# Retention and a squared-ReLU FFN on one core: from a batch at a time to 36 units of 128 tokens with FFN groups of 512

## The chip, the core and the metric

The kernel runs on one core of a Trainium2 chip. The metric is device time in microseconds. Before the change it is 639.69 us, the median of 3 runs (639.65 to 640.98). Five engines work side by side, each on its own queue of instructions in program order: TensorE (PE, with its weight loads shown apart as PEld), VectorE (DVE), ScalarE (ACT), GpSimd (POOL) and SyncE (SP), which here only issues DMAs.

## The reference

Eight batches of eight heads, 576 tokens, head size 64. Retention has no softmax: scores are multiplied by a decay that falls with the distance of the tokens. An FFN with a squared ReLU follows on all 4608 tokens.

```python
gamma = 1.0 - 2.0 ** (-5.0 - np.arange(H))
Dmat = np.where(rel >= 0, gamma[:, None, None] ** rel, 0.0)   # rel = i - j
ret = (q @ k.T / sqrt(64) * Dmat) @ v                          # per batch and head
x = ret.transpose(0, 2, 1, 3).reshape(4608, 512)
h = x @ w_in                                                   # 512 -> 2048
out = (np.maximum(h, 0) ** 2) @ w_out                          # 2048 -> 512
```

## The kernel before

Everything is computed in fp16 with fp32 sums in PSUM. The retention is done in chunks of 128 tokens: inside a chunk by masked scores, across chunks by a 64x64 state per head.

The loop over the 8 batches (L100) has three stages.

1. **Retention** (L103 to L197), one head at a time. Six DMAs load q, k and v of the head with runs of 256 bytes (L110 to L122). ACT and DVE cast them and multiply q and k by their decays (L124 to L143). PE transposes q and k together, five matmuls (L150); ACT copies qT out (L153) and DVE kT (L154). Five score matmuls follow (L165), four state matmuls (L170), the mask on DVE (L174) with the running state (L179, L181), and per chunk an output matmul from the masked scores (L188) and one from the state (L192) with ACT's copy into xT (L195). A head has 64 rows, so most of these matmuls use half of PE's rows or half of its columns.
2. **FFN1** (L201 to L213): 16 blocks of 128 hidden columns times two halves of 288 tokens, four matmuls each (L205); ACT takes the ReLU (L210), POOL squares it (L212).
3. **FFN2** (L215 to L226): five token tiles, 16 matmuls of 512 columns each (L219), DVE's copy (L224), and a DMA of SP (L225).

A scheduler places the instructions; on PE the stages follow one another, save that the next head's transposes and the next stage's first matmuls begin a little early. The weights are loaded in fp32 through SP and cast by POOL (L90) and DVE (L97) at the start, beside the first heads.

Of the kernel before, what the change touches and what calls it, by code (L numbers as in the profile page):

```python
# [8 lines left out]
FP32 = mybir.dt.float32  # L9
FP16 = mybir.dt.float16  # L10


@with_exitstack
def kernel(
# [5 lines left out]
    moe_w_in: bass.AP,  # L20
    moe_w_out: bass.AP,
    out: bass.AP,
):
    nc = tc.nc
    B, H, S, D = q.shape
    DM, DFF = moe_w_in.shape
    assert (B, H, S, D) == (8, 8, 576, 64)
    scale = 1.0 / math.sqrt(D)

    NQ = 288  # L30
    n_kt = (S + 127) // 128
    n_ic = S // NQ
    n_f = DFF // 128
    n_dm = DM // 128
    n_tt = (S + 127) // 128
    C = 128

    const_pool = ctx.enter_context(tc.tile_pool(name="const", bufs=1))
    w_pool = ctx.enter_context(tc.tile_pool(name="w", bufs=1))
    stage_pool = ctx.enter_context(tc.tile_pool(name="stage", bufs=2))  # L40
    qk_pool = ctx.enter_context(tc.tile_pool(name="qk", bufs=3))
    work_pool = ctx.enter_context(tc.tile_pool(name="work", bufs=2))
    big_pool = ctx.enter_context(tc.tile_pool(name="big", bufs=1))
    psum_pool = ctx.enter_context(tc.tile_pool(name="psum", bufs=8, space=bass.MemoryType.PSUM))

    identity_h = const_pool.tile([128, 128], FP16, name="identity_h")
    make_identity(nc, identity_h)

    iota_p = const_pool.tile([128, 1], FP32, name="iota_p")
    nc.gpsimd.iota(iota_p, pattern=[[0, 1]], base=0, channel_multiplier=1,  # L50
                   allow_small_or_imprecise_dtypes=True)
    one_p = const_pool.tile([128, 1], FP32, name="one_p")
    nc.vector.memset(one_p, 1.0)

    qdecay = []
    kdecay = []
    dmask = []
    gummas = []
    for h in range(H):
        gamma = 1.0 - 2.0 ** (-5.0 - h)  # L60
        lng = math.log(gamma)
        gummas.append(gamma)
        qd = const_pool.tile([128, 1], FP32, name=f"qdecay{h}")
        kd = const_pool.tile([128, 1], FP32, name=f"kdecay{h}")
        mbias = stage_pool.tile([128, 1], FP32, name=f"mb{h}", tag="mb")
        nc.vector.memset(mbias, math.log(scale))
        nc.scalar.activation(out=qd, in_=iota_p,
                             func=mybir.ActivationFunctionType.Exp,
                             bias=mbias, scale=lng)
        mbias2 = stage_pool.tile([128, 1], FP32, name=f"mb2{h}", tag="mb")  # L70
        nc.vector.memset(mbias2, 128.0 * lng)
        nc.scalar.activation(out=kd, in_=iota_p,  # L72
                             func=mybir.ActivationFunctionType.Exp,
                             bias=mbias2, scale=-lng)
        dm_t = const_pool.tile([128, C], FP32, name=f"dmask{h}")
        nc.gpsimd.memset(dm_t, gamma ** -128)
        nc.gpsimd.affine_select(
            out=dm_t, in_=dm_t, compare_op=mybir.AluOpType.is_ge, fill=0.0,
            base=0, pattern=[[1, C]], channel_multiplier=-1,
        )  # L80
        qdecay.append(qd)
        kdecay.append(kd)
        dmask.append(dm_t)

    w_in_h = []
    for dm in range(n_dm):
        st = stage_pool.tile([128, DFF], FP32, name=f"w_in_st{dm}", tag="wst")
        nc.sync.dma_start(out=st, in_=moe_w_in[dm * 128:(dm + 1) * 128, :])
        t = w_pool.tile([128, DFF], FP16, name=f"w_in{dm}")
        nc.gpsimd.tensor_copy(out=t, in_=st)  # L90
        w_in_h.append(t)
    w_out_h = []
    for f in range(n_f):
        st = stage_pool.tile([128, DM], FP32, name=f"w_out_st{f}", tag="wst2")
        nc.sync.dma_start(out=st, in_=moe_w_out[f * 128:(f + 1) * 128, :])
        t = w_pool.tile([128, DM], FP16, name=f"w_out{f}")
        nc.vector.tensor_copy(out=t, in_=st)  # L97
        w_out_h.append(t)
# [158 lines left out]
```

## Time and profile before

The table is from one profiled execution, taken on the only core. Its span, from first to last instruction, is 638.2 us; an own end-to-end time of that execution is not listed. The median of the timed runs, 639.69 us, is 1.5 us above the span.

| | PE | PEld | DVE | ACT | POOL |
|---|---|---|---|---|---|
| busy us | 517.0 | 299.2 | 201.4 | 303.6 | 172.7 |
| share of the span | 81% | 47% | 32% | 48% | 27% |
| instructions | 3136 | 3136 | 841 | 913 | 283 |

The chain of work that ended last runs 58% through PE, 22% through POOL, 7% through ACT and 6% through DVE. DMA moved 46.76 MB, 73 GB/s over the span; 117696 of its 124913 packets are under 512 bytes.

PE's busy time counts each matmul from its start to its modelled end, so overlapping matmuls in a row are merged and a busy PE need not stream columns at its peak. Mean times of one matmul therefore hold a fixed tail; how fast a row of matmuls goes is read from a timeline row: its length less the mean of the last one, over the count less one.

### The profile page before, as it was taken

What the parts mean: (1) busy time and instruction counts of PE and PEld (TensorE: products, weight loads), DVE (VectorE), ACT (ScalarE), POOL (GpSimd) and SP (SyncE); (2) the same over time, 40 slices, a digit from 0 to 9 for tenths busy, and PEclk for the clock granted to TensorE, in tenths of its full rate; (3) what the DMA queues carried; (4) which work ended last, traced back from release to release, by engine and by line L of the source; (5) the groups of instructions that cost most, each with busy time, mean ns of one, the idle gap of its engine ahead of it and who ended that gap; (6) DMA issues with size and microseconds to landing.
All of it is one profiled execution on the core that took longest, in us unless ns stands there. A gap on an engine that the chain in (4) does not pass through costs nothing.

```text
span 638.2 us, 9634 instructions
## 1 busy us (share of the span) xinstructions
PE 517.0 (81%) x3136; PEld 299.2 (47%) x3136; DVE 201.4 (32%) x841; ACT 303.6 (48%) x913; POOL 172.7 (27%) x283
## 2 busy tenths in 40 slices
PE   0357998779977899779987799877997789977997
PEld 0234644447444564446544475444744446444563
DVE  2555114440154302551035501444015530254101
ACT  3255733566146660566425563366614566055450
POOL 4200750009200290005700075000930019000380
PEclk9999998559975599557995579755997559965699
DMA  7765502430133301432024310233113330120001
GB/s 286 230 162 125 115 35 69 91 86 20 50 81 84 85 1 66 91 86 57 17 67 94 90 32 34 69 85 90 24 49 76 90 84 1 66 66 0 1 13 62
DMA packets 124913, 46.76 MB, mean 73 GB/s; under 512 B 117696, under 2 KB 117696, under 8 KB 124352
## 3 DMA queue, kind: packets, MB, share of 16 engines
q1 hardware_dynamic: 124864, 46.17, 27.7%
q8 instruction: 24, 0.39, 0.3%
q14 instruction: 25, 0.20, 0.1%
HBM read 36.70 MB, written 9.44 MB: 72 GB/s over the span
## 4 chain that ended last, share of the span: by engine, by line
PE 58%; POOL 22%; ACT 7%; DVE 6%; DMA 4%; issue 2%; ACTq 0%; SPq 0%; DVEq 0%
POOL gT L212 22%; PE pout L219 18%; PE pout L188 9%; PE pout L192 8%; PE ps_sc L165 7%; PE ptr L150 7%; ACT qT L153 6%; PE ph L205 5%; DVE kT L154 5%; PE ps_st L170 3%; DMA w_out_st<-in_moe_w_out_dram 3%; DVE w_out L97 1%; ACT r L210 1%; DMA qk<-in_k_dram 1%; DVE retT L174 0%
## 5 line engine op out<-in xcount | busy, mean ns | idle before, releaser
L212 POOL TENSOR_TENSOR gT<-r 128x288 f16<-128x288 f16 x256 | 161.2, 670 | 438.9 <-ACT r L210 438.3
L219 PE MATMUL pout<-w_out,gT 128*128 128x512 f16 (+1 forms) x640 | 142.9, 380 | 7.5 <-POOL gT L212 6.9
L205 PE MATMUL ph<-xT,w_in 128*128 128x288 f16 x1024 | 143.2, 306 | 0.0
L210 ACT ACTIVATE r<-ph 128x288 f16<-128x288 f32 x256 | 105.3, 411 | 59.7 <-POOL gT L212 41.6
L205 PEld LDWEIGHTS <-w_in 128*128 128x128 f16 x1024 | 104.9, 104 | 33.0
L165 PE MATMUL ps_sc<-qT,kT 64*128 64x128 f16 (+1 forms) x320 | 48.9, 286 | 80.9 <-DVE kT L154 79.6
L224 DVE COPY o<-pout 128x512 f32<-128x512 f32 (+1 forms) x40 | 27.6, 690 | 270.5 <-PE pout L219 270.5
L219 PEld LDWEIGHTS <-gT 128*128 128x128 f16 (+1 forms) x640 | 62.8, 100 | 85.5 <-POOL gT L212 13.6
L153 ACT COPY qT<-ptr 64x576 f16<-64x576 f16 x64 | 40.5, 632 | 129.9 <-PE ptr L150 129.4
L188 PE MATMUL pout<-retT,vh 128*64 128x128 f16 (+1 forms) x320 | 90.1, 282 | 3.2 <-ACT xT L195 0.7
L195 ACT CAST xT<-pout 64x128 f16<-64x128 f32 (+1 forms) x320 | 75.0, 246 | 33.5 <-PE pout L188 19.1
L174 DVE TENSOR_TENSOR retT<-ps_sc,dmask 128x128 f16<-128x128 f32 (+1 forms) x320 | 79.8, 266 | 24.5 <-PE ps_sc L165 24.5
L150 PE MATMUL ptr<-identity_h,qkh 128*128 128x128 f16 (+1 forms) x320 | 55.5, 274 | 25.5 <-ACT kdecay L72 13.0
L165 PEld LDWEIGHTS <-kT 64*128 64x128 f16 (+1 forms) x320 | 28.7, 123 | 101.0 <-DVE kT L154 89.0
L192 PE MATMUL pout<-qT,state 64*64 64x128 f16 (+1 forms) x256 | 73.9, 292 | 0.0
L128 ACT ACTIVATE qkh<-qk,qdecay 128x256 f16<-128x256 f32 x64 | 32.4, 507 | 82.6 <-PE ps_st L170 82.5
L154 DVE COPY kT<-ptr 64x576 f16<-64x576 f16 x64 | 29.4, 459 | 106.2 <-ACT qT L153 106.2
L192 PEld LDWEIGHTS <-state 64*64 64x64 f16 x256 | 31.8, 124 | 50.3 <-issue 33.5
L150 PEld LDWEIGHTS <-qkh 128*128 128x128 f16 (+1 forms) x320 | 27.1, 113 | 45.2 <-issue 16.1
L188 PEld LDWEIGHTS <-vh 128*64 128x64 f16 (+1 forms) x320 | 39.0, 140 | 15.5 <-DVE retT L174 0.3
L181 DVE SCALAR_TENSOR_TENSOR state<-state,ps_st 64x64 f16<-64x64 f16 x192 | 39.6, 206 | 0.0
L170 PE MATMUL ps_st<-vh,qkh 128*64 128x64 f16 x256 | 26.3, 241 | 0.0
(24 smaller groups left out, 160.7 us busy)
## 6 DMA issues: line engine op xcount, KB each, us to landing
qk<-in_q_dram SPq DMA_DIRECT2D x64, 128.0 KB, 2.3
qk<-in_k_dram SPq DMA_DIRECT2D x64, 128.0 KB, 2.5
v<-in_v_dram SPq DMA_DIRECT2D x64, 128.0 KB, 2.4
out_dram<-o SPq DMA_DIRECT2D x32, 256.0 KB, 2.0
w_in_st<-in_moe_w_in_dram SPq DMA_DIRECT2D x4, 1024.0 KB, 5.9
w_out_st<-in_moe_w_out_dram SPq DMA_DIRECT2D x16, 256.0 KB, 2.9
qk<-in_q_dram SPq DMA_DIRECT2D x64, 16.0 KB, 2.2
qk<-in_k_dram SPq DMA_DIRECT2D x64, 16.0 KB, 2.2
```

The source lines that it names most:

```text
L150: nc.tensor.transpose(ptr[:, st * C:st * C + slen], qkh_sb[0:slen, st, :], identity_h[0:slen, 0:slen])
L153: nc.scalar.copy(out=qT_h, in_=ptr[0:64, :])
L154: nc.vector.tensor_copy(out=kT_h, in_=ptr[64:128, :])
L165: nc.tensor.matmul(ps_sc[i][0:L, 0:L], lhsT=kT_h[:, i * C:i * C + L], rhs=qT_h[:, i * C:i * C + L], start=True, stop=True)
L174: nc.vector.tensor_tensor(out=retT[0:L, i * C:i * C + L], in0=ps_sc[i][0:L, 0:L], in1=dmask[h][0:L, 0:L], op=mybir.AluOpType.mult)
L188: nc.tensor.matmul(pout[:, 0:L], lhsT=vh_sb[0:L, i, :], rhs=retT[0:L, i * C:i * C + L], start=True, stop=(i == 0))
L192: nc.tensor.matmul(pout[:, 0:L], lhsT=states[i - 1], rhs=qT_h[:, i * C:i * C + L], start=False, stop=True)
L195: nc.scalar.copy(out=xT_h[dm][hodd * 64:hodd * 64 + 64, i * C:i * C + L], in_=pout[:, 0:L])
L205: nc.tensor.matmul(ph, lhsT=w_in_h[dm][:, f * 128:(f + 1) * 128], rhs=xT_h[dm][:, ic * NQ:ic * NQ + NQ], start=(dm == 0), stop=(dm == n_dm ...
L210: nc.scalar.activation(out=r_sb, in_=ph, func=mybir.ActivationFunctionType.Relu)
L212: nc.gpsimd.tensor_tensor(out=gT_sb[f][:, ic * NQ:ic * NQ + NQ], in0=r_sb, in1=r_sb, op=mybir.AluOpType.mult)
L219: nc.tensor.matmul(pout[0:tlen, :], lhsT=gT_sb[f][:, t * 128:t * 128 + tlen], rhs=w_out_h[f], start=(f == 0), stop=(f == n_f - 1))
```

## The change

The kernel is rewritten. The work is cut into 36 units of 128 tokens of all 8 heads: four full chunks per batch, and one tail unit for two batches, which holds the last 64 tokens of each. Four units make a group of 512 tokens, and there are 9 groups.

A unit's retention works on pairs of heads, so that stationary operands are 128x128. kT is kept twice with the other head's rows zeroed (`kTs`), v is padded with zero columns (`vps`), and the state of a pair is a 128x128 matrix whose off-diagonal blocks the constant `bdec` zeroes. The decay moves: v is multiplied on POOL, the mask is 0 or 1, and the query side's decay is multiplied in when the output leaves PSUM (`gam`). Each unit has 8 transposes, 8 scores, 4 state matmuls (none in a tail) and, per pair, 2 output matmuls and 1 from the state (none in a batch's first chunk, 2 of 64 columns in a tail).

POOL casts k and q; ACT copies kT out of PSUM in two halves; DVE copies qT, masks four score blocks at a time, carries the state and squares the ReLU. The FFN output is copied by ACT and sent by ACT's DMA queue. The weights come by eight DMAs of POOL's queue that cast to fp16 on the way.

The order is written out by hand (`manual_schedule`): the four units of group 0 first, one after the other; then, for each group, its 64 FFN1 and 64 FFN2 matmuls, and between them the retention of the next group's units, each unit within 32 FFN matmuls: one transpose, score or state matmul after an FFN matmul, three output matmuls after each from the 27th on. Removed lines are those printed above; the core of the new ones:

```diff
+    units = []
+    for bp in range(B // 2):
+        for b in (2 * bp, 2 * bp + 1):
+            units += [("full", b, c) for c in range(4)]
+        units.append(("tail", 2 * bp, 4))
+    NU = len(units)
+    UPG = 4
+    NG = NU // UPG
...
+    ld = ctx.enter_context(tc.tile_pool(name="ld", bufs=5))
+    cast = ctx.enter_context(tc.tile_pool(name="cast", bufs=3))
+    work = ctx.enter_context(tc.tile_pool(name="work", bufs=2))
+    st_pool = ctx.enter_context(tc.tile_pool(name="st", bufs=4))
...
+    ps_ff = ctx.enter_context(tc.tile_pool(name="ps_ff", bufs=3, space=bass.MemoryType.PSUM))
+    ps_sc = ctx.enter_context(tc.tile_pool(name="ps_sc", bufs=2, space=bass.MemoryType.PSUM))
+    ps_one = ctx.enter_context(tc.tile_pool(name="ps_one", bufs=1, space=bass.MemoryType.PSUM))
+    ctx.enter_context(tc.manual_schedule())
...
+    def load(u):
+        kind, b, c = units[u]
+        t = {}
+        for name, src in (("q", q), ("k", k), ("v", v)):
+            x = ld.tile([P, H, D], FP32, name=f"{name}32", tag=f"{name}32")
+            if kind == "full":
+                nc.sync.dma_start(out=x, in_=src[b, :, c * P:(c + 1) * P, :].rearrange("h p d -> p h d"))
+            else:
+                for i in range(2):
+                    nc.sync.dma_start(out=x[i * 64:(i + 1) * 64],
+                                      in_=src[b + i, :, 512:576, :].rearrange("h p d -> p h d"))
+            t[name] = x
+        loaded[u] = t
...
+    for u in range(4):
+        load(u)
+    for fb in range(4):
+        nc.gpsimd.dma_start(out=w_in16[:, :, fb * 512:(fb + 1) * 512],
+                            in_=w_in[:, fb * 512:(fb + 1) * 512].rearrange("(m p) f -> p m f", p=P))
+    for fb in range(4):
+        nc.gpsimd.dma_start(out=w_out16[:, fb * 4:(fb + 1) * 4, :],
+                            in_=w_out[fb * 512:(fb + 1) * 512, :].rearrange("(n p) m -> p n m", p=P))
...
+    ident = const.tile([P, P], FP16, name="ident")
+    make_identity(nc, ident)
...
+        m = const.tile([P, P], FP32, name=f"mask_{kind}")
+        nc.gpsimd.memset(m, 1.0)
+        nc.gpsimd.affine_select(out=m, in_=m, compare_op=ALU.is_ge, fill=0.0,
+                                base=0, pattern=[[1, P]], channel_multiplier=-1)
...
+        t = const.tile([P, NP, 192], FP16, name=f"vp{i}")
+        nc.vector.memset(t[:, :, 64:128], 0.0)
+        vps.append(t)
+        t = const.tile([P, NP, 2, P], FP16, name=f"kTb{i}")
+        nc.vector.memset(t[64:128, :, 0, :], 0.0)
+        nc.vector.memset(t[0:64, :, 1, :], 0.0)
...
+        nc.gpsimd.tensor_copy(out=k16, in_=t["k"].rearrange("p h d -> p (h d)"))
+        nc.gpsimd.tensor_copy(out=q16, in_=t["q"].rearrange("p h d -> p (h d)"))
+        vp = vps[u % NB]
+        vo = vp.rearrange("p n (a d) -> p n a d", d=64)[:, :, 0:3:2, :]
+        nc.gpsimd.tensor_tensor(
+            out=vo,
+            in0=t["v"].rearrange("p (n a) d -> p n a d", a=2),
+            in1=vdec[kind].rearrange("p (n a o) -> p n a o", a=2, o=1).to_broadcast([P, NP, 2, D]),
+            op=ALU.mult)
...
+                    nc.tensor.transpose(ps[:, i, hp, :], r[src][:, hp * P:(hp + 1) * P], ident)
+                    if hp == NP - 1:
+                        if i == 1:
+                            kT = kTs[u % NB]
+                            qT = work.tile([P, NP, P], FP16, name="qT", tag="qT")
+                            nc.scalar.copy(out=kT[0:64, :, 0, :], in_=ps[0:64, 0])
+                            nc.scalar.copy(out=kT[64:128, :, 1, :], in_=ps[64:128, 0])
+                            nc.vector.tensor_copy(out=qT, in_=ps[:, 1])
...
+                    if hp % 2 == 0 and a == 0:
+                        r["psc"] = ps_sc.tile([P, 2, 2, P], FP32, name="psc", tag="psc")
+                    nc.tensor.matmul(r["psc"][:, hp % 2, a, :], lhsT=r["kT"][:, hp, a, :],
+                                     rhs=r["qT"][:, hp, :], start=True, stop=True)
+                    if hp % 2 == 1 and a == 1:
+                        nc.vector.tensor_tensor(
+                            out=rT[:, hp - 1:hp + 1].rearrange("p n a i -> p (n a) i"),
+                            in0=r["psc"].rearrange("p n a i -> p (n a) i"),
+                            in1=mask[kind].rearrange("p (o i) -> p o i", o=1).to_broadcast([P, 4, P]),
+                            op=ALU.mult)
...
+                    if c == 0:
+                        nc.vector.tensor_tensor(out=Rn, in0=psf, in1=bdec, op=ALU.mult)
+                    else:
+                        tmp = work.tile([P, NP, P], FP32, name="stmp", tag="stmp")
+                        nc.vector.tensor_tensor(out=tmp, in0=psf, in1=R[b], op=ALU.add)
+                        nc.vector.tensor_tensor(out=Rn, in0=tmp, in1=bdec, op=ALU.mult)
...
+        inter = [] if c == 0 else ([(0, P, R[b])] if kind == "full" else [(0, 64, R[b]), (64, P, R[b + 1])])
...
+                    nc.tensor.matmul(r["psO"][:, hp, :], lhsT=r["vp"][:, hp, a * 64:a * 64 + P],
+                                     rhs=r["rT"][:, hp, a, :], start=(a == 0),
+                                     stop=(a == 1 and not inter))
...
+                    nc.tensor.matmul(r["psO"][:, hp, lo:hi], lhsT=Rb[:, hp, :], rhs=r["qT"][:, hp, lo:hi],
+                                     start=False, stop=last)
...
+            nc.vector.tensor_tensor(out=xTs[g][:, :, s * P:(s + 1) * P], in0=r["psO"], in1=gam[kind], op=ALU.mult)
...
+                    nc.tensor.matmul(cur["ph"], lhsT=w_in16[:, m, f * P:(f + 1) * P], rhs=xTs[g][:, m, :],
+                                     start=(m == 0), stop=(m == NP - 1))
+                    if m == NP - 1:
+                        gT.append(g_pool.tile([P, UPG * P], FP16, name=f"gT{f}", tag=f"gT{f}"))
+                        rl = r_pool.tile([P, UPG * P], FP16, name="rl", tag="rl")
+                        nc.scalar.activation(out=rl, in_=cur["ph"], func=ACTF.Relu)
+                        nc.vector.tensor_tensor(out=gT[f], in0=rl, in1=rl, op=ALU.mult)
...
+                    nc.tensor.matmul(cur["po"], lhsT=gT[f][:, t * P:(t + 1) * P], rhs=w_out16[:, f, :],
+                                     start=(f == 0), stop=(f == NF - 1))
+                    if f == NF - 1:
+                        o = work.tile([P, DM], FP32, name="o", tag="o")
+                        nc.scalar.copy(out=o, in_=cur["po"])
+                        if kind == "full":
+                            r0 = b * S + c * P
+                            nc.scalar.dma_start(out=out[r0:r0 + P, :], in_=o)
...
+    for u in range(UPG):
+        cast_unit(u)
+        run(steps_T(u))
+        run(steps_score(u))
+        run(steps_state(u))
+        run(steps_out(u))
+    for g in range(NG):
+        nxt = [u for u in range((g + 1) * UPG, (g + 2) * UPG) if u < NU]
+        wide = 2 * NF * UPG
+        per = wide // UPG
+        w_steps = steps_ff1(g)
+        w2 = None
+        queue = []
+        for i in range(wide):
+            if i == NF * NP:
+                w_steps += steps_ff2(g)
+            slot, ph = divmod(i, per)
+            if nxt:
+                if ph == 0:
+                    u = nxt[slot]
+                    load(u)
+                    cast_unit(u)
+                if ph == 2:
+                    queue += steps_T(nxt[slot])
+                if ph == 14:
+                    queue += steps_score(nxt[slot])
+                    queue += steps_state(nxt[slot])
+                if ph == 27:
+                    queue += steps_out(nxt[slot])
+            w_steps[i]()
+            if queue:
+                queue.pop(0)()
+            if ph >= 27 and queue:
+                queue.pop(0)()
+                if queue:
+                    queue.pop(0)()
+        run(queue)
```

On PE, before, the end of a head: the last output matmuls of a head from the masked scores (vh) and from the state, and behind them the next head's first transpose.

```order
L188 LDWEIGHTS vh
L188 MATMUL pout<-retT,vh 64x64
L192 LDWEIGHTS state_517
L192 MATMUL pout<-qT,state_517 64x64
L150 LDWEIGHTS qkh
L150 MATMUL ptr<-identity_h,qkh 128x128
```

On PE now, in the first group's FFN2 (po, from gT and w_out): a state matmul (psS) of the next group's unit stands between two FFN matmuls.

```order
L310 LDWEIGHTS gT_515
L310 MATMUL po<-w_out_88,gT_515 128x512
L229 LDWEIGHTS k_777
L229 MATMUL psS<-vp_191,k_777 128x128
L310 LDWEIGHTS gT_535
L310 MATMUL po<-w_out_88,gT_535 128x512
```

Retention matmuls stood in chains of their own; now FFN matmuls of 512 columns lie between them, of the group before.

On PE now, at the end of that group: the last unit's last output matmuls (psO), the group's last FFN2 matmul (po), and the next group's first FFN1 matmul, which waits for DVE's xT.

```order
L257 LDWEIGHTS vp_191
L257 MATMUL psO<-rT,vp_191 128x128
L263 LDWEIGHTS R
L263 MATMUL psO<-qT,R 128x128
L310 LDWEIGHTS gT_667
L310 MATMUL po<-w_out_88,gT_667 128x512
L290 LDWEIGHTS w_in_87
L290 MATMUL ph<-xT,w_in_87 128x512 [waits DVE_49]
```

Between the output that DVE must turn into xT and the matmul that reads it stands one FFN2 matmul.

On POOL, before, the constants come first and the casts of the weights wait for SP's DMAs; the end of the constants:

```order
L77 AFFINE_SELECT dmask_159<-dmask_159 128x128 [waits Pool_49]
L77 AFFINE_SELECT dmask_170<-dmask_170 128x128 [waits Pool_49]
L90 CAST w_in_175<-w_in_st_173 128x2048 [waits DMAHW0_49]
L90 CAST w_in_179<-w_in_st_177 128x2048 [waits DMAHW1_49]
L90 CAST w_in_183<-w_in_st_181 128x2048 [waits DMAHW0_49]
```

On POOL now, the start: the eight weight DMAs, then the constants (ident is what the transposes need), then the first unit's casts.

```order
L82 DMA w_in_87<-in_moe_w_in_dram 128x4x512 x4
L85 DMA w_out_88<-in_moe_w_out_dram 128x4x512 x4
masks.py:197 MEMSET ident 128x128
masks.py:199 ISA
masks.py:199 AFFINE_SELECT ident<-ident 128x128 [waits Pool_49]
L92 IOTA iota_p 128x1
L95 IOTA iota_f 128x128
```

The identity, and with it the first transpose, has moved behind eight DMA issues on the same queue.

## Rows read from the trace of the kernel before

**Rows 1.** Page, part 2: TensorE's granted clock in tenths, 40 slices

```profile
PEclk9999998559975599557995579755997559965699
```

**Rows 2.** Stages of a batch: window, length, busy per engine, clock, DMA, GB/s

```profile
253.52:292.71 39.19, 28.83 (x184) 16.22 (x184) 21.21 (x97) 23.21 (x76) 0.00 (x0) 0.56 0.37 83
292.71:310.05 17.34, 17.34 (x131) 13.02 (x130) 0.00 (x0) 11.42 (x30) 14.98 (x24) 0.92 0.12 26
310.05:328.86 18.81, 17.83 (x82) 7.77 (x80) 2.77 (x4) 2.88 (x7) 5.12 (x9) 1.00 0.15 57
```

**Rows 3.** Waits: who <- for whom: us in total, times, longest

```profile
ACT r L210 <- POOL gT L212: 41.6, 193, 0.3
PE ps_sc L165 <- DVE kT L154: 79.6, 63, 1.6
```

**Rows 4.** Groups by shape: busy us, mean ns of one | idle before, releasers

```profile
L212 POOL TENSOR_TENSOR gT<-r 128x288 f16<-128x288 f16 x256 | 161.2, 670 | 438.9 <-ACT r L210 438.3
L219 PE MATMUL pout<-w_out,gT 128*128 128x512 f16 x512 | 114.4, 379 | 7.5 <-POOL gT L212 6.9
L210 ACT ACTIVATE r<-ph 128x288 f16<-128x288 f32 x256 | 105.3, 411 | 59.7 <-POOL gT L212 41.6 <-PE ph L205 17.2
L195 ACT CAST xT<-pout 64x128 f16<-64x128 f32 x256 | 62.6, 256 | 28.2 <-PE pout L188 19.1 <-PE pout L192 6.8
L153 ACT COPY qT<-ptr 64x576 f16<-64x576 f16 x64 | 40.5, 632 | 129.9 <-PE ptr L150 129.4
L154 DVE COPY kT<-ptr 64x576 f16<-64x576 f16 x64 | 29.4, 459 | 106.2 <-ACT qT L153 106.2
L224 DVE COPY o<-pout 128x512 f32<-128x512 f32 x32 | 22.1, 692 | 247.5 <-PE pout L219 247.5
L90 POOL CAST w_in<-w_in_st 128x2048 f16<-128x2048 f32 x4 | 7.6, 1894 | 8.1 <-DMA w_in_st<-in_moe_w_in_dram 8.1
```

**Rows 5.** Timeline, PE in both FFN stages: start, us, engine, line, count

```profile
299.82 3.35 PE L205 MATMUL ph<-xT,w_in 128*128 128x288 f16 x26
...
325.74 3.18 PE L219 MATMUL pout<-w_out,gT 128*64 128x512 f16 x14
```

**Rows 6.** Timeline, a batch's first two heads, clock 1.00, then 0.50

```profile
328.86 0.53 PE L150 MATMUL ptr<-identity_h,qkh 128*128 128x128 f16 x5
...
329.42 0.63 ACT L153 COPY qT<-ptr 64x576 f16<-64x576 f16 x1 [15.05 <-PE ptr L150]
330.09 0.46 DVE L154 COPY kT<-ptr 64x576 f16<-64x576 f16 x1 [0.44 <-ACT qT L153]
...
330.60 0.54 PE L165 MATMUL ps_sc<-qT,kT 64*128 64x128 f16 x5 [1.22 <-DVE kT L154]
...
334.73 0.79 PE L165 MATMUL ps_sc<-qT,kT 64*128 64x128 f16 x5 [1.22 <-DVE kT L154]
```

**Rows 7.** Groups by shape, 328.5 to 329.5 us: last of five transposes

```profile
L150 PE MATMUL ptr<-identity_h,qkh 64*128 64x64 f16 x1 | 0.2, 200 | 0.0
```

**Rows 8.** Timeline of the first 23 us

```profile
0.80 0.87 SPq L88 DMA_DIRECT2D w_in_st<-in_moe_w_in_dram  x2
...
8.19 1.90 POOL L90 CAST w_in<-w_in_st 128x2048 f16<-128x2048 f32 x1 [0.59 <-DMA w_in_st<-in_moe_w_in_dram]
8.81 1.56 DVE L97 CAST w_out<-w_out_st 128x512 f16<-128x512 f32 x1 [7.82 <-DMA w_out_st<-in_moe_w_out_dram]
...
10.76 0.42 DVE L97 CAST w_out<-w_out_st 128x512 f16<-128x512 f32 x1 [0.38 <-issue]
...
22.56 0.79 PE L165 MATMUL ps_sc<-qT,kT 64*128 64x128 f16 x5 [1.22 <-DVE kT L154]
```

**Rows 9.** Stretches with loads: columns as in rows 2

```profile
2.00:13.00 11.00, 0.00 (x0) 0.00 (x1) 2.61 (x13) 3.31 (x14) 6.32 (x15) 1.00 0.86 299
334.00:336.00 2.00, 1.25 (x10) 0.85 (x11) 1.20 (x5) 0.42 (x3) 0.00 (x0) 0.50 0.58 129
```

**Rows 10.** Timeline, the last copy before the span ends

```profile
634.11 0.68 DVE L224 COPY o<-pout 64x512 f32<-64x512 f32 x1 [2.88 <-PE pout L219]
```

More of the change, by code (lines that the diff above doesn't have):

```diff
@@ L42 @@
[L42 to L49, printed above, removed]
+    DM, DFF = w_in.shape
+    assert (B, H, S, D, DM, DFF) == (8, 8, 576, 64, 512, 2048)
+    P = 128
@@ new lines @@
+    gam_f = const.tile([P, NP, P], FP32, name="gam_full")
+    gam_t = const.tile([P, NP, P], FP32, name="gam_tail")
+    for hp in range(NP):
+        nc.scalar.activation(out=gam_f[:, hp, :], in_=iota_f, func=ACTF.Exp, scale=lncol[:, hp:hp + 1])
+    nc.vector.tensor_copy(out=gam_t[:, :, 0:64], in_=gam_f[:, :, 0:64])
+    nc.vector.tensor_copy(out=gam_t[:, :, 64:128], in_=gam_f[:, :, 0:64])
+    gam = {"full": gam_f, "tail": gam_t}
+    bdec = const.tile([P, NP, P], FP32, name="bdec")
+    nc.vector.memset(bdec, 0.0)
@@ new lines, in steps_score, with f @@
+    def steps_score(u):
+        kind = units[u][0]
+        r = ret[u]
+        steps = []
+        for hp in range(NP):
+            for a in range(2):
+                def f(hp=hp, a=a):
+                    if hp == 0 and a == 0:
+                        r["rT"] = work.tile([P, NP, 2, P], FP16, name="rT", tag="rT")
+                    rT = r["rT"]
+                    if hp % 2 == 0 and a == 0:
[8 more added lines that the diff above has]
+                            op=ALU.mult)
+                steps.append(f)
+        return steps
@@ new lines, in steps_ff2, with s @@
+    def steps_ff2(g):
+        gT = gTs[g]
+        steps = []
+        cur = {}
+        for t in range(UPG):
+            kind, b, c = units[g * UPG + t]
+            for f in range(NF):
+                def s(t=t, f=f, kind=kind, b=b, c=c):
+                    if f == 0:
+                        cur["po"] = ps_ff.tile([P, DM], FP32, name="po", tag="ff")
+                    nc.tensor.matmul(cur["po"], lhsT=gT[f][:, t * P:(t + 1) * P], rhs=w_out16[:, f, :],
[6 more added lines that the diff above has]
+                            nc.scalar.dma_start(out=out[r0:r0 + P, :], in_=o)
+                        else:
+                            for i in range(2):
+                                r0 = (b + i) * S + 512
+                                nc.scalar.dma_start(out=out[r0:r0 + 64, :], in_=o[i * 64:(i + 1) * 64])
+                steps.append(s)
+        return steps
@@ new lines, in run @@
+    def run(steps):
+        for s in steps:
+            s()
+    for u in range(UPG):
[35 more added lines that the diff above has]
+        run(queue)
```

301 lines of the change are left out of this document (122 added, 179 removed).

## The prediction

> **What bounds the kernel now.** I read the granted clock first, then busy time by stage, then who waits for whom, and last the timeline for prices.
>
> The clock falls and rises eight times [rows 1]; one dip is one batch's retention. By stage [rows 2] a batch takes 75.3 us: 39.2 of retention at a mean clock of 0.56, 17.3 of FFN1 at 0.92 and 18.8 of FFN2 at 1.00. In retention PE counts as busy for 28.8 of 39.2 us, yet no other engine is busier: it is a chain of handoffs. The wait that shows it is score matmuls waiting for DVE's kT, 79.6 us over 63 heads, 1.26 us each [rows 3]. In one head the transposes end at 329.39, ACT copies until 330.05, DVE until 330.55, and PE goes on at 330.60 [rows 6]. The same five scores take 0.54 us at clock 1.00 and 0.79 at 0.50 [rows 6]. At 22.56 us they take 0.79 too [rows 8] though the first slices print full clock, so I read the start-up as the lower level. FFN1 is paced by POOL: 32 squares of 0.670 are 21.4 us against PE's 17.3 [rows 2, 4], and ReLUs wait for them 193 times [rows 3].
>
> So of the eight batches' 603 us, 314 are retention chains and 289 are FFN.
>
> **What the change costs on PE.** FFN: 9 groups of 128 matmuls, all of 512 columns, 1152 in all. Fourteen such took 3.18 us, the last one 0.379 by its mean: (3.18 - 0.379) / 13 = 0.2154 us each [rows 4, 5]. 1152 x 0.2154 = **248.1**.
>
> Retention: 8 units with 28 matmuls (a batch's first chunk), 24 with 32, 4 tails with 32: 1120 of 128 columns or fewer. Group 0's 124 run in the start-up; 996 lie between FFN matmuls. At full clock five transposes, each with its own weight load, took 0.53, the last 0.20 [rows 6, 7]: (0.53 - 0.20) / 4 = 0.0825. From below, 128 columns at the FFN rate are 0.054 (the weight load wholly hidden); from above, five scores at the lower level are 0.79 / 5 = 0.158. A short one stands behind a 512-column one that hides its load, but the next FFN matmul's load must fit under the short one; this is what the five transposes do, so I take 0.0825: 996 x 0.0825 = **82.2** (54 to 157).
>
> [...] The fourteen FFN matmuls at full clock go at 0.2154 each [rows 5]. [...]
>
> **What stands beside PE.** A group takes PE 27.6 + 10.3 = 37.8 us, its FFN1 half 18.9. Prices of the others by the nearest rows [rows 4]:
> - ACT: 16 ReLUs of 512. Its slope is (632 - 256) / 448 = 0.84 ns an element, so 0.411 + 224 x 0.84 ns = 0.60; two kT copies a unit, 0.632 - 64 x 0.84 ns = 0.58 each. FFN1 half with two units: 9.6 + 2.3 = 11.9. FFN2's four copies and DMA issues are less.
> - DVE: a unit has the qT copy (0.459 x 512 / 576 = 0.41) and up to five operations of 512 fp32 elements at L224's 0.69: 3.9. A square of 512 fp16 is not shown; with L154's 16-bit rate it is 0.41, with L224's 0.69. Types decide, so I take 0.41. FFN1 half: 14.3 (18.8 with 0.69).
> - POOL: two casts by L90's rate, 0.47 each, and one product of two inputs by L212's rate, 1.19: 2.1 a unit, 8.5 a group.
> All fit under PE. The squares leave POOL, so its 0.670 no longer paces FFN1; what is late next is PE itself.
>
> Three handoffs can still stop PE. (1) From transposes to scores stand five FFN matmuls, 1.08 us, and ACT's first copy needs about 0.2 + 0.6; the second score needs the second copy, at about 1.35 us against PE's 1.4. The margin is thin and a ReLU (0.60) may stand ahead in ACT's queue: 0 to 0.6 a unit; the order puts the ReLU two FFN matmuls earlier, so I take 0.1, 32 x 0.1 = **3.2** (0 to 19). (2) From scores to output matmuls lie the state matmuls and an FFN matmul, over 1.3 us, against one mask of 0.69: nothing; without that cover 0.7 a unit. (3) At each of 8 group ends the last output goes through DVE into xT: 0.20 + 0.03 + 0.69 + 0.05, less the 0.30 that PE still has to do: 0.7, **5.6** in all. Nothing else on PE is queued around it.
>
> **The two ends.** Start-up: four units' q, k, v are 3.15 MB. In retention 0.58 of the DMA engines moved 129 GB/s [rows 9], so 222 at full share: 14.2 us. The weights are 8.39 MB; at 299 GB/s for 0.86 [rows 9], 348, they take 24.1. Two queues share the engines, so the four units are in after 0.8 + 28.4 = 29.2. The last unit then needs two casts (0.95), its chain (a head's 39.2 / 8 = 4.9) and xT (1.0): FFN starts at **36**. From below: with q, k, v first, unit 0 is in at 4.4, and four chains end at 26. From above: POOL issues eight DMAs that cast, which no row shows, ahead of the identity that the transposes need; SP issues a 1 MB DMA in 0.43 [rows 8], so eight take 3.5, but if POOL were held until all 38.3 us of transfers were done, the start would be at 61. I take the transfers' value, which lies between. FFN1 begins at the lower clock: 17.3 x (1 - 0.92) = **1.4** [rows 2].
> Tail: ACT's copy 0.60, then what followed the last copy before, 638.2 - 634.79 = 3.4 [rows 10], and one more DMA issue of 0.43, since the last unit is a tail: **4.6** with the rest of the last matmul.
>
> Sum: 36 + 1.4 + 248.1 + 82.2 + 3.2 + 5.6 + 4.6 = 381.1, against the profiled span of 638.2. The median of the runs is 1.5 above that span; with the same 1.5, **383**.
>
> **Rivals.**
> A. Weight loads hide wholly and a short matmul costs its columns: 0.054, so 28.5 less, **354**. For it: in FFN1 26 matmuls of 288 columns took 3.35, 0.129 each at most, so loads hide there [rows 5]. Against: the five transposes.
> B. POOL's queue is held by its casting DMAs and the start slips to 61: **408**. For it: eight DMAs ahead of everything, and no row of such a DMA. Against: SP's issues cost 0.43.
> C. ACT's queue exposes the first handoff: ReLUs stand before the kT copies, and each of 32 units pays the 1.26 that each head pays now: **423**. Against: five FFN matmuls in between, as ordered.
> D. DVE paces FFN1. A cast of DVE took 1.56 us while POOL was casting, and 0.42 alone [rows 8]. [...] If squares cost 0.69 and all POOL work of a half stands in DVE's way, the half is 18.8 + 4.3 = 23.1 instead of 18.9: 8 x 4.2 = 34 more, **417**. Against: POOL is busy 8.5 of 37.8 us, so few operations meet.
> E. The clock stays low. Matmuls in a chain kept it at 0.50, and short ones are now in every stretch. If all PE work cost twice, the time would be 383 + 330 = **713**, slower than before; it decides from 0.78 of the work at the lower level. Against: with PE filled without a gap FFN2 had 1.00 [rows 2], and here no gap is over 1 us.
> F. The new order does not overlap at all, retention chains between FFN groups: 36 chains of 4.9 and 248 are about 430. The order shows FFN matmuls between the steps, so this is only C at its worst.
>
> **Numbers.** Forecast (PE bound, 366 to 400): 0.59. A 0.10, B 0.12, C and F 0.10, D 0.07, E 0.02. The range leaves out E, the worst of C and F, and the low end of A: **352 to 424**. A difference under 0.2% could not be told from no change here. Faster 0.97, within 0.2% 0.01, slower 0.02: only E comes near.
>
> **What would show it.** Right: PE busy without gaps between about 36 us and the end, clock 1.00 there; ten or so short gaps of 0.7 before L290 waiting for DVE's xT; a group period near 38 us; L296 near 0.41. A period of 34 to 35 means A; scores (L204) waiting for ACT by 1 us mean C; ACT's ReLUs waiting for DVE mean D; first transposes later than 15 us behind POOL mean B. I am wrong above all if the short matmul between two long ones costs something other than 0.08.

## The result and the profile after

The changed kernel takes 391.5 us (median of 4 runs, 390.69 to 392.92) against 639.93 before (4 runs, one more than the 3 behind 639.69): ratio 0.612, 95% interval 0.610 to 0.613. The forecast was 383, the range 352 to 424. The profiled execution took 392.92 us with a span of 391.2.

The page of the changed kernel, parts 1 and 2 (each digit is a tenth in one of 40 slices):

```profile
PE 327.6 (84%) x2272; PEld 181.1 (46%) x2272; DVE 204.5 (52%) x385; ACT 151.7 (39%) x259; POOL 92.8 (24%) x129
...
PE   0304699998999899989989998999899989998995
...
PEclk9999999999999999999999999999999999999998
```

The dips of [rows 1] are gone. That row shows seven, where the prediction counts eight: the first batch's retention lies in the start-up, whose slices print full clock though a row of scores takes 0.79 us there [rows 8]. Here, too, the first slices don't tell: the first FFN1 matmuls start 0.427 us apart. From 54 us to the tail the granted clock is at its upper level (1.00 in the window of 100 to 330 us below, where FFN matmuls start 0.216 us apart), and PE is busy in nearly every slice from the sixth on. No stage runs at 0.56 any more as the retention of [rows 2] did.

Waits of the changed kernel (who <- for whom: us in total, times, longest us):

```profile
DVE qT L187 <- ACT kTb L186: 68.8, 35, 11.6
...
PE psc L204 <- DVE qT L187: 30.8, 36, 4.7
...
ACT rl L295 <- DVE gT L296: 18.6, 38, 0.5
...
PE ph L290 <- DVE xT L270: 5.5, 9, 1.2
```

These answer to [rows 3]. ReLUs waiting for squares fell from 41.6 to 18.6 us, and PE's wait at the first score from 79.6 to 30.8. The 30.8 is the largest wait of PE, and the first row says what stands behind it: DVE's copy of qT waits for ACT's second copy of kT.

Groups by shape of the changed kernel (busy us, mean ns of one | idle before, releasers):

```profile
L295 ACT ACTIVATE rl<-ph 128x512 f16<-128x512 f32 x144 | 86.0, 597 | 72.8 <-PE ph L290 53.8 <-DVE gT L296 18.6
L296 DVE TENSOR_TENSOR gT<-rl 128x512 f16<-128x512 f16 x144 | 72.7, 509 | 47.3 <-ACT rl L295 44.8
...
L164 POOL TENSOR_TENSOR vp<-v,vdec_full 128x512 f16<-128x512 f32 x32 | 34.9, 1090 | 34.2 <-PE psO L257 18.2 <-DMA v<-in_v_dram 9.1 <-PE psO L263 6.2
...
L239 DVE TENSOR_TENSOR R<-stmp,bdec 128x512 f16<-128x512 f32 x24 | 23.0, 960 | 0.8
L161 POOL CAST q<-q 128x512 f16<-128x512 f32 x36 | 22.7, 630 | 1.2 <-PE psT L180 0.9 <-DMA k<-in_k_dram 0.3
```

The prices worked out from [rows 4] for ACT (0.60) and POOL's product (1.19) were near; POOL's cast of q takes 0.63 for 0.47, the square 0.51 for 0.41, the state's product 0.96 for 0.69.

**Where the time stands.** I took the time from each PE matmul's start to the next one's start, over the whole trace. An FFN matmul takes 0.216 us and a short one 0.056 (0.028 with 64 columns); what is longer is a stall. The sums make up the span:

| term | predicted | measured |
|---|---|---|
| start-up, until the first FFN1 matmul | 36 | 49.0 |
| FFN1's start at the lower clock | 1.4 | 2.5 |
| 1152 FFN matmuls | 248.1 | 248.4 |
| 996 short matmuls | 82.2 | 54.7 |
| 32 stalls from transposes to scores | 3.2 | 26.1 |
| 8 group ends | 5.6 | 5.6 |
| tail | 4.6 | 4.9 |
| sum | 381.1 | 391.2 |

So the total is near because an error of -27.5 in one term met errors of +22.9 and +13.0 in two others. The experiments go at these three.

Timeline of the changed kernel, one handoff in FFN2 (start, us, engine, line, operation, count, idle before):

```profile
82.43 0.22 PE L180 MATMUL psT<-ident,q 128*128 128x128 f16 x1
82.48 1.24 PE L310 MATMUL po<-w_out,gT 128*128 128x512 f16 x5
84.38 0.22 PE L204 MATMUL psc<-qT,kTb 128*128 128x128 f16 x1 [0.65 <-DVE qT L187]
...
82.68 0.58 ACT L185 COPY kTb<-psT 64x512 f16<-64x512 f16 x1 [2.02 <-PE psT L180]
83.28 0.58 ACT L186 COPY kTb<-psT 64x512 f16<-64x512 f16 x1
...
83.90 0.42 DVE L187 COPY qT<-psT 128x512 f16<-128x512 f16 x1 [3.34 <-ACT kTb L186]
```

The FFN matmul behind the last transpose starts 0.056 us after it. The transpose starts at 82.43, the first score at 84.38: 1.95 us, where 0.056 and five FFN matmuls cover 1.14. Three copies run one after the other, two of ACT and then DVE's, all out of the tile psT. The stall is 0.81 us, 32 times.

Timeline of SP's queue in the start-up:

```profile
2.69 0.93 SPq L68 DMA_DIRECT2D q<-in_q_dram  x1
3.66 7.13 SPq L68 DMA_DIRECT2D k<-in_k_dram  x1
10.84 6.47 SPq L68 DMA_DIRECT2D v<-in_v_dram  x1
17.34 6.47 SPq L68 DMA_DIRECT2D q<-in_q_dram  x1
23.85 6.24 SPq L68 DMA_DIRECT2D k<-in_k_dram  x1
30.13 3.52 SPq L68 DMA_DIRECT2D v<-in_v_dram  x1
33.70 0.98 SPq L68 DMA_DIRECT2D q<-in_q_dram  x1
```

And the DMA queues from 8 to 28 us (packets, MB, share of 16 engines):

```profile
q0 software_dynamic: 3143, 3.12, 91.8%
q1 hardware_dynamic: 3136, 0.79, 29.9%
```

q0 carries the weights, q1 carries q, k and v. Both move the same number of packets, 3143 and 3136, and within 3 of each other in every 4 us of this window; but a weight packet writes 992 bytes and one of q, k, v 252. So the weights get four fifths of what is written, and the loads of the first units come at 40 GB/s. SP's issue of 256 KB stretches from 0.93 us to between 6.2 and 7.1 while this lasts.

What followed, timeline of POOL and PE: unit 1's v, the first transposes of units 2 and 3, and the first FFN1 matmul.

```profile
34.00 1.04 POOL L164 TENSOR_TENSOR vp<-v,vdec_full 128x512 f16<-128x512 f32 x1 [4.96 <-DMA v<-in_v_dram]
...
36.76 0.63 PE L180 MATMUL psT<-ident,k 128*128 128x128 f16 x4
...
42.14 0.63 PE L180 MATMUL psT<-ident,k 128*128 128x128 f16 x4
...
49.02 1.44 PE L290 MATMUL ph<-xT,w_in 128*128 128x512 f16 x3 [1.22 <-DVE xT L270]
```

### The profile page after: what moved, and what is told of

It is laid out like the page before. It is cut to its first block, busy times and chain, and to the rows that moved or that the text cites. A ratio compares the mean times of both kernels' runs of the same rounds, so it can differ in the third digit from the quotient of the medians.

```text
span 391.2 us, 5966 instructions
## 1 busy us (share of the span) xinstructions
PE 327.6 (84%) x2272; PEld 181.1 (46%) x2272; DVE 204.5 (52%) x385; ACT 151.7 (39%) x259; POOL 92.8 (24%) x129
## 4 chain that ended last, share of the span: by engine, by line
PE 64%; DVE 11%; ACT 10%; DMA 7%; issue 4%; SPq 3%; POOL 0%; ACTq 0%
PE ph L290 25%; PE po L310 24%; DMA v<-in_v_dram 6%; PE psc L204 5%; ACT kTb L186 5%; DVE qT L187 4%; ACT rl L295 4%; PE psO L257 4%; PE psT L180 3%; SPq L68 3%; DVE gT L296 2%; PE psS L229 2%; DVE R L239 2%; DMA out_dram<-o 2%; DVE xT L270 2%
## 5 line engine op out<-in xcount | busy, mean ns | idle before, releaser
L290 PE MATMUL ph<-xT,w_in 128*128 128x512 f16 x576 | 157.1, 383 | 5.5 <-DVE xT L270 5.5
L310 PE MATMUL po<-w_out,gT 128*128 128x512 f16 x576 | 154.4, 379 | 0.0
L295 ACT ACTIVATE rl<-ph 128x512 f16<-128x512 f32 x144 | 86.0, 597 | 72.8 <-PE ph L290 53.8
L296 DVE TENSOR_TENSOR gT<-rl 128x512 f16<-128x512 f16 x144 | 72.7, 509 | 47.3 <-ACT rl L295 44.8
L290 PEld LDWEIGHTS <-w_in 128*128 128x128 f16 x576 | 55.0, 99 | 76.1 <-issue 25.4
L310 PEld LDWEIGHTS <-gT 128*128 128x128 f16 x576 | 54.4, 98 | 68.0 <-issue 14.9
L204 PE MATMUL psc<-qT,kTb 128*128 128x128 f16 x288 | 60.0, 228 | 30.8 <-DVE qT L187 30.8
L207 DVE TENSOR_TENSOR rT<-psc,mask_full 128x512 f16<-128x512 f32 x64 | 43.6, 687 | 24.0 <-PE psc L204 24.0
L187 DVE COPY qT<-psT 128x512 f16<-128x512 f16 x36 | 15.2, 423 | 68.8 <-ACT kTb L186 68.8
L164 POOL TENSOR_TENSOR vp<-v,vdec_full 128x512 f16<-128x512 f32 x32 | 34.9, 1090 | 34.2 <-PE psO L257 18.2
L257 PE MATMUL psO<-rT,vp 128*128 128x128 f16 x288 | 39.9, 229 | 0.0
```

Source lines behind the costliest of these rows:

```text
L164: nc.gpsimd.tensor_tensor(out=vo, in0=t["v"].rearrange("p (n a) d -> p n a d", a=2), in1=vdec[kind].rearrange("p (n a o) -> p n a o", a=2, ...
L187: nc.vector.tensor_copy(out=qT, in_=ps[:, 1])
L204: nc.tensor.matmul(r["psc"][:, hp % 2, a, :], lhsT=r["kT"][:, hp, a, :], rhs=r["qT"][:, hp, :], start=True, stop=True)
L207: nc.vector.tensor_tensor(out=rT[:, hp - 1:hp + 1].rearrange("p n a i -> p (n a) i"), in0=r["psc"].rearrange("p n a i -> p (n a) i"), in1= ...
L257: nc.tensor.matmul(r["psO"][:, hp, :], lhsT=r["vp"][:, hp, a * 64:a * 64 + P], rhs=r["rT"][:, hp, a, :], start=(a == 0), stop=(a == 1 and ...
L290: nc.tensor.matmul(cur["ph"], lhsT=w_in16[:, m, f * P:(f + 1) * P], rhs=xTs[g][:, m, :], start=(m == 0), stop=(m == NP - 1))
```

## The experiments

Times are medians of the runs of one kernel, ratios those to the kernel before of the same session. "Stalls" are summed from the starts of matmuls as above.

**1. q in a PSUM tile of its own.** Theory: the two engines wait because they read one tile. Rival: DVE's place in its queue, or ACT's copies as such.

```diff
-                    if i == 0 and hp == 0:
-                        r["psT"] = ps_one.tile([P, 2, NP, P], FP16, name="psT", tag="psT")
+                    if hp == 0:
+                        if i == 0:
+                            r["psT"] = ps_one.tile([P, 2, NP, P], FP16, name="psT", tag="psT")
+                        else:
+                            r["psT"] = ps_sc.tile([P, 2, NP, P], FP16, name="psq", tag="psc")
```

The copies of kT are issued after the fourth transpose, that of qT after the eighth.

> The q transposes get a PSUM tile of their own (a buffer of the score tiles), the k transposes keep theirs; nothing else changes. In the changed kernel PE stands still before each unit's first score, 32 times 0.81 us = 26.1 us outside the start-up, until DVE has copied qT. Theory 1: DVE is late because its copy may only follow ACT's two kT copies (0.58 us each) out of the same PSUM tile, so ACT and DVE work one after the other. Then the 26.1 us go: about 364 us (362 to 368), and scores wait for nothing. Rival: DVE is late because of the squares in its own queue; then at least 0.4 us of each stall stays, 378 us or more.

Measured: 374.19 us, ratio 0.585 (0.583 to 0.586), between the two. The 13.0 us of stalls in the FFN2 halves are gone, down to nothing; of the 13.0 in the FFN1 halves 11.2 stayed. That is 14.9 of the 19.9 us by which the spans of the two profiled executions differ (the medians differ by 17.3). The other 5.0 are start-up: FFN1 starts at 46.5 instead of 49.0, and at the upper clock, which gives 2.5. The timeline of this kernel in an FFN1 half says why:

```profile
93.70 0.60 ACT L300 ACTIVATE rl<-ph 128x512 f16<-128x512 f32 x1 [0.49 <-PE ph L295]
94.30 0.58 ACT L187 COPY kTb<-psT 64x512 f16<-64x512 f16 x1
94.90 0.58 ACT L188 COPY kTb<-psT 64x512 f16<-64x512 f16 x1
95.51 1.08 ACT L300 ACTIVATE rl<-ph 128x512 f16<-128x512 f32 x2
...
96.14 0.42 DVE L301 TENSOR_TENSOR gT<-rl 128x512 f16<-128x512 f16 x1 [1.06 <-ACT rl L300]
96.48 0.42 DVE L192 COPY qT<-psq 128x512 f16<-128x512 f16 x1
...
96.95 0.22 PE L209 MATMUL psc<-qT,kTb 128*128 128x128 f16 x1 [0.52 <-DVE qT L192]
```

DVE's copy no longer waits for its data but for its turn: it stands behind a square, the square waits for a ReLU, and that ReLU stands behind ACT's copies of kT. So both theories held, each in one half. The edit does two things at once, though: it parts the tiles, and it lets ACT copy kT four FFN matmuls earlier. What each is worth alone was not tried. That ACT and DVE took turns at the shared tile is seen in the records: in the changed kernel DVE's copy of qT starts 31 to 33 ns after the end of ACT's second copy in 35 of 36 units, and beside an ACT copy of kT in none; here it runs beside one in 19.

**2. More cover.** Transposes two FFN matmuls earlier, scores two later (`ph == 2` to 0, `ph == 14` to 16).

> The PSUM tile stays shared, but transposes begin two FFN matmuls earlier and scores two later: 9 instead of 5 FFN matmuls in between, 0.86 us more cover. Theory 1 (a chain of fixed length, 0.2 + 0.58 + 0.6 + 0.42 us, that lacks 0.81 us of cover): the stalls before the scores go, 26.1 us, and about 2 us come back at the group ends because the outputs end later: 367 us (364 to 371). Rival (DVE's queue, not the chain): the wait moves with the scores and more than half of the 26 us stays, 380 or more.

Measured: 375.53 us, 0.587 (0.586 to 0.588), 8 above what was expected and 4 above the end of its range. The stalls at the scores fall from 26.1 to 6.3 (5.9 of it in FFN1 halves). But a unit ends later: the group ends rise from 5.6 to 7.6, and 1.4 us are lost at output matmuls. Cover taken at one end of a slot of 32 is missing at its other end.

**3. q first.** As 1, and q is transposed before k, so that DVE's copy stands four steps earlier in DVE's queue.

```diff
-        for i, src in enumerate(("k16", "q16")):
+        for i, src in enumerate(("q16", "k16")):
```

> As with the PSUM tiles apart (374.2), and besides q is transposed before k, so that DVE's copy of q is asked for four steps earlier, ahead of the ReLU and the square of that place. Theory, the 11.2 us of stalls that were left there in the FFN1 halves are DVE's copy of q standing behind a square that waits for a ReLU that waits behind ACT's copies of k: they go, 374.2 - 11.2 = about 363 (361 to 367); what is late next is ACT's second copy of k. Rival, the stalls are ACT's own queue (ReLU and two copies of k, 1.76 us against 1.36 of cover): they stay at 0.4 to 0.7 a unit, 370 to 375.

Measured: 368.69 us, 0.576 (0.575 to 0.578). The stalls in FFN1 are down from 11.2 to 1.5, those in FFN2 are 1.4: the mechanism is the theory's. The time is 5.7 above its figure and 1.7 above its range: the start-up was 1.6 us longer than in 1, FFN1 began at the lower clock (2.4 us), and 2.9 us of stalls are left.

**4. The price of a short matmul.** Each score matmul is issued twice (`for _ in range(2):` around it).

> Every score matmul is issued twice; the second writes the same block again. 32 units x 8 = 256 more 128-column matmuls lie between FFN matmuls (group 0's 32 are in the start-up, where loads set the pace, about 1 us). Theory, a short matmul between two long ones costs its columns, 0.056 us as the start-to-start times of the changed kernel show: 256 x 0.056 = 14.3, so 391.5 + 14.3 + 1 = about 407 (405 to 409). Rival, the 0.0825 of the prediction is the price of a further short one and something else made the changed kernel cheaper: 21.1 more, 413 to 415.

Measured: 406.27 us, 0.635 (0.634 to 0.636). In the trace 1252 short matmuls take 68.8 us in place of 54.7 for 996: 14.1 more for 256, 0.055 each. The stalls at scores stay at 26.1. A short matmul between long ones cost 0.055 us here, what 128 columns at the FFN's rate come to (0.054); 0.0825 is refuted.

**5. No interleaving.** The next group's retention comes after the group's FFN:

```diff
-            if queue:
-                queue.pop(0)()
...
+        for u in nxt:
+            cast_unit(u)
+            run(steps_T(u))
+            run(steps_score(u))
+            run(steps_state(u))
+            run(steps_out(u))
```

> The four units of the next group are cast and worked through after a group's 128 FFN matmuls instead of between them; the loads are still asked for at the same places. Theory, the gain of the change comes mainly from laying the handoffs of the retention under FFN matmuls: a unit's chain by itself takes about 5.4 us, as the units of group 0 do in the start-up, so 32 x 5.4 = 173 in place of 55 of short matmuls, 26 of stalls and 6 of group ends, and some 2 us for each of 8 starts of FFN1 at the lower clock: 391.5 + 173 - 87 + 14 = about 492 (475 to 520). Rival, the pairing of heads and the other cuts carry the gain and order gives little: chains overlap with each other, 3 us a unit, so about 415 (400 to 430).

Measured: 494.68 us, 0.773 (0.772 to 0.775). In the trace a group is on average 16.2 us of FFN1, 13.8 of FFN2 and 21.2 of retention, 5.3 a unit; FFN1 is 2.4 above its 64 x 0.216. So of the 248 us gained in all, 103 hang on the order and 145 on the rest (pairs of heads, longer matmuls, fewer and larger copies, squares off POOL), which no run takes apart. Dips of the clock are back, shallower than those of [rows 1]; seen in the windows of one FFN and, for the most part, one retention (length, then busy us of PE, PEld, DVE, ACT, POOL, then clock, DMA share, GB/s):

```profile
49.00:77.00 28.00, 27.99 (x119) 12.13 (x118) 7.57 (x16) 11.31 (x19) 3.03 (x4) 0.91 0.99 170
77.00:100.00 23.00, 13.46 (x135) 10.79 (x134) 13.28 (x23) 5.22 (x9) 8.97 (x12) 0.82 0.55 127
```

**6. w_out later.** Its four DMAs are issued after the casts of unit 3.

> The four DMAs of w_out are issued after the casts of group 0's last unit instead of at the start; w_in stays at the start. Theory 2: the DMA engines take one packet of each queue in turn, so the 256-byte packets of q, k, v get 40 GB/s beside the 1 KB packets of the weights (156 GB/s) until the weights are in, and FFN1 starts at 49 us because units 1 to 3 come late. With half the weights, unit 1 is in at about 20 instead of 34 us, FFN1 starts at about 35, and the time is about 377 us (374 to 381). Rival, as the prediction had it: both queues get equal time on the engines, so q, k, v are in at the same time whatever half of the weights does: 389 or more.

Measured: 383.53 us, 0.599 (0.598 to 0.600). FFN1 starts at 39.0 instead of 49.0, and the span is shorter by 10.2: the gain is the start-up's. The start lies 4 us above the one expected, the time 2.5 above the range.

**7. All weights later**, at that same place.

> All eight weight DMAs are issued after the casts of group 0's last unit. Theory 2: q, k, v of group 0 come at some 220 GB/s, POOL's and DVE's constants are 6 us earlier, the start-up is set by four chains of 5.4 us, and FFN1 starts at about 30 us: 372 us (369 to 378). It could be spoiled by FFN1 waiting for the late w_in (it would show as PE waiting for that DMA). Rival (equal shares): FFN1 can't start before all weights and loads, 38 us of transfers, have mostly passed: 385 or more.

Measured: 378.87 us, 0.592 (0.591 to 0.593), 0.9 above the range. FFN1 starts at 29.1, as expected, but one score of unit 7 stalls for 6.3 us, and the clock falls there for a while: PEclk prints 6 in the slice of 66.0 to 75.5 us. Timeline of this kernel:

```profile
28.91 6.42 SPq L68 DMA_DIRECT2D v<-in_v_dram  x1
35.42 6.42 SPq L68 DMA_DIRECT2D q<-in_q_dram  x1
...
52.90 0.58 ACT L308 COPY o<-po 128x512 f32<-128x512 f32 x1 [0.98 <-PE po L304]
59.13 0.38 ACTq L311 DMA_DIRECT2D out_dram<-o  x1
59.55 0.58 ACT L308 COPY o<-po 128x512 f32<-128x512 f32 x1 [6.07 <-DMA q<-in_q_dram]
65.33 0.34 ACTq L311 DMA_DIRECT2D out_dram<-o  x1
65.72 0.58 ACT L179 COPY kTb<-psT 64x512 f16<-64x512 f16 x1 [5.58 <-DMA v<-in_v_dram]
```

SP's issues stretch again, now from 22 to 50 us, to between 3.7 and 6.8 us each. When the weights are through, SP catches up with its loads, and ACT's output DMAs, ready at 53.5 and 60.1, are issued at 59.13 and 65.33; ACT's copy of kT stands behind them. That the one delays the other I read from the order of time; it was not tried by itself.

**8. Outputs earlier.** As 3, two scores or states after an FFN matmul instead of one, outputs from the 24th instead of the 27th.

> As with q first, and besides two score or state matmuls after an FFN matmul instead of one, and the output matmuls from the 24th FFN matmul of a slot instead of the 27th, so that DVE's last product is ready before a group ends. Theory, the 0.73 us at each of 8 group ends is that product exposed: it goes, about 6 us less than with q first, 357 (354 to 361). Rival, outputs now come before the masks are through and wait for DVE, 0.3 to 0.7 a unit: 10 to 22 us more than with q first.

Measured: 369.96 us, 0.578 (0.577 to 0.579), 13 above the theory and not faster than 3. The group ends do fall, from 5.6 to 0.9. But 9.8 us are lost at a place that neither theory named, the second score. Timeline of this kernel:

```profile
97.53 0.58 ACT L188 COPY kTb<-psT 64x512 f16<-64x512 f16 x1
97.80 0.59 PE L209 MATMUL psc<-qT,kTb 128*128 128x128 f16 x2
...
98.16 0.10 PEld L209 LDWEIGHTS <-kTb 128*128 128x128 f16 x1 [0.47 <-ACT kTb L188]
```

The second score reads the second half of kT. The FFN matmul between the first and the second had covered ACT's second copy; without it PE waits 0.30 us, 32 times.

**9. The first two scores single, then pairs.** As 8, with transposes from the 1st FFN matmul and pairs only from the 16th:

```diff
-                if ph == 2:
+                if ph == 1:
...
+            for _ in range(1 if ph < 16 else 2 if ph < 24 else 3):
```

> As with q first, with three numbers of the table of steps changed: transposes from the 1st FFN matmul of a slot instead of the 2nd, after the first two scores two steps for each FFN matmul, outputs from the 24th instead of the 27th. Theory, the first two score matmuls need five and six FFN matmuls of cover behind the last transpose and then nothing waits: the 9.8 us that the run with early outputs lost at its second score go, the 5 us at the group ends go, and so do 2.9 us left at the first score: 368.7 - 4.7 - 2.9 = about 361 (359 to 363). Rival, what the group ends give comes back elsewhere, since DVE has the work of a unit in less time: 366 to 370.

Measured: 360.78 us, 0.564 (0.563 to 0.565), as the theory had it. From the first FFN1 matmul on, stalls and lower clock together are 3.8 us, 34.2 in the changed kernel. The windows of 100 to 330 us, of this kernel:

```profile
100.00:330.00 230.00, 229.65 (x1671) 128.27 (x1669) 141.63 (x249) 103.99 (x181) 56.84 (x71) 1.00 0.39 98
```

and of the changed kernel:

```profile
100.00:330.00 230.00, 211.39 (x1512) 115.98 (x1511) 134.47 (x230) 98.71 (x169) 56.33 (x73) 1.00 0.40 95
```

PE is busy for 229.65 of 230 us, with 1671 matmuls where the changed kernel did 1512. This is the bound that the forecast spoke of.

**10. The best.** As 9, and w_in is issued after the casts of unit 3, w_out after those of unit 6.

> As with the changed table of steps, and w_in is asked for after the casts of unit 3, w_out after those of unit 6, so that q, k and v do not take turns with the weights before FFN1 starts. Theory: FFN1 starts at 29 instead of 47 to 49, as in the run with all weights late; 361 - 18 = 343, plus up to 5 us of waits for w_out or for unit 6 or 7, since all transfers up to there take about 50 us of the 16 engines: 346 (342 to 351). Rival: the wait of 6.5 us that the run with all weights late showed at one score, behind an output DMA of ACT that was issued 5.6 us late, comes more than once: 350 to 356.

Measured: 351.79 us, 0.550 (0.548 to 0.552): faster than both kernels, 39.7 us under the changed one. FFN1 starts at 27.8. The time is 0.8 above the theory's range and inside the rival's, but for a reason that the theory named and sized too small; the waits of this kernel:

```profile
PE po L317 <- DMA w_out<-in_moe_w_out_dram: 7.0, 4, 2.4
```

and the window around them:

```profile
45.00:60.00 15.00, 8.01 (x31) 3.16 (x29) 3.53 (x7) 2.01 (x4) 3.19 (x4) 0.67 1.20 202
```

FFN2 of group 0 waits four times for w_out, once for each of its DMAs, and over this window the granted clock is a mean 0.67: from 51.9 us on a matmul of 512 columns is followed after 0.38 to 0.43 us instead of 0.22, which is the lower level. The rival's stall of 6.5 us at a score doesn't come. Stalls and lower clock after the start of FFN1 are 14.2 us, against 3.8 in run 9. What is left is transfers: the last of w_out lands at 58.1 us, and the DMA engines are full in the whole window.

## Why the prediction was right, and where it was wrong

**Right: the bound.** PE is busy for 211 of the 230 us from 100 to 330 us, the clock stays up (rival E, 713 us, is out), and the FFN term was exact: 0.2154 from [rows 4, 5] against 0.216. Group ends (5.6) and tail were right too. D cost nothing that shows on PE: 38 of 144 squares met an operation of POOL and ACT waited 18.6 us for squares, but no FFN matmul stalled.

**Luck: how near 383 came.** Three terms were wrong, by -27.5, +22.9 and +13.0, and the signs happened to differ. The sign of being right that was to tell the prices of a short matmul apart came out by the same luck: from its second group on the changed kernel's period is 38.1 to 38.8 us, near the 38 of the forecast, but 34.5 of it are matmuls at 0.216 and 0.056 and the rest is stalls. The 34 to 35 that was to mean A shows only in run 9 (34.4 to 35.2 from the second group on), where the stalls are gone.

**Wrong: 82.2 for the short matmuls; rival A's price is the true one.** The step that failed is (0.53 - 0.20) / 4 = 0.0825 from [rows 6, 7]. It takes five transposes as alike, but the fifth is another shape: 64 rows, 64 columns. The records of the five in [rows 6] start 66, 56, 56 and then 151 ns apart. The first four ran at 0.056; the wait before the odd one carried the average. The five scores behind them do the same, 65, 56, 56 and then 146 ns: there, too, the fifth has another shape (64 columns), and all five read tiles that one copy each had filled, so late data is not the cause. The row that gave the right answer was the bound from below, 128 columns at the FFN's rate, 0.054, and run 4 shows 0.055.

**Wrong: 3.2 for the handoff; it was 26.1.** The step said that ACT's first copy frees the first score. It left out DVE's copy of qT, which the same score needs and which starts only when ACT's second copy out of the tile has ended. [Rows 4] had it: DVE's kT waited 106.2 us for ACT's qT, and in [rows 6] ACT's copy ends at 330.05, DVE's begins at 330.09. I had used these rows for prices and not for the order. In the changed kernel's timeline the steps in this order take 0.25 + 0.60 + 0.62 + 0.48 = 1.95 against 1.14 of cover, which is 0.81. In the changed kernel's trace the copies of ACT and DVE out of that one tile overlap in none of 36 units, with tiles apart in 19 (run 1) and 11 (run 9). Rival C had the right place and named the wrong queue; its 1.26 a unit was 0.81.

**Wrong: 36 for the start-up; it was 49.0.** The step that failed is that two queues share the engines evenly and the four units are in after 29.2. It gave q, k and v half of the engines' time, half of 222 GB/s, until they were in. They got 40, packet for packet with the weights, their packets a quarter as large. So when the weights were in, at 33.8 us, only unit 0 had all its tiles; unit 1's v came at 33.9, and unit 3's last tile landed at 40.2. From 34.0 on PE had the rest of unit 1 (2.8 us), the chains of units 2 and 3 (5.4 each) and the wait for xT (1.5): 49.0. Runs 6 and 7 moved the start to 39.0 and 29.1 by issuing weights later and nothing else; the size of the packets was not varied, so that the share goes by packets rests on the counts, 3143 beside 3136. Rival B's cause, POOL held by its casting DMAs, was wrong: eight issues took 6.2 us, and the first cast ran at 9.48.

## What to carry to other kernels

Before the cost of a short instruction is taken from a merged row, look whether all its members have one shape; the mean over an odd one was half too high here, 0.0825 for 0.056. For each handoff follow every operand of the waiting instruction, and read from the trace of before not only how long its copies take but whether two engines take turns at one tile. Two transfers in different queues shared the engines by packets here (3143 beside 3136), and the one with 252 bytes in a packet got 40 GB/s beside 156: what is needed first should be asked for before the large one.

## What the runs showed of the hardware

- **DVE and POOL held each other up here, and the one that started first kept its time.** In the changed kernel 106 squares met no operation of POOL and took 0.423 us; 16 that began during a product of POOL took 1.09; 14 that began before a cast of POOL took 0.43, and that cast 0.82 instead of 0.61. The state's product took 0.96 there and 0.70 in run 5, though POOL worked beside 21 of 24 in run 5 too: 12 of these began before POOL's product, which then took 1.43 instead of 1.04. Both operations of DVE read two inputs from SBUF; the mask (L207), which reads PSUM, took 0.69 in the 2 that met POOL and the 70 that did not, and xT's product (L270), which reads PSUM too, 0.69 in 22 and 0.68 in 14. In the changed kernel:

```profile
88.26 0.61 POOL L161 CAST q<-q 128x512 f16<-128x512 f32 x1
...
88.34 1.07 DVE L239 TENSOR_TENSOR R<-stmp,bdec 128x512 f16<-128x512 f32 x1
```

In run 5, where all squares but one ran without POOL:

```profile
L296 DVE TENSOR_TENSOR gT<-rl 128x512 f16<-128x512 f16 x144 | 62.0, 431 | 95.4 <-ACT rl L295 95.4
...
L239 DVE TENSOR_TENSOR R<-stmp,bdec 128x512 f16<-128x512 f32 x24 | 16.8, 699 | 0.8
```

- **Weight loads cost no time of their own here.** Every short matmul had its own weight load, recorded at about 0.10 us, and so had every long one; the starts still lie 0.056 and 0.216 us apart, also where the two kinds alternate.
- **A DMA's issue held its queue here.** SP's issue of 256 KB took 0.4 to 1.3 us (once 2.0) in the changed kernel's first 50 us, but 6.2 to 7.1 for four in a row beside the weights and 3.5 for the one during which the weights ended.
